# Causal attention with decay and a two-layer mixer on one core: decay rows in the score matmul, exp over whole PSUM banks, mixer groups of 512 tokens

## The chip, the cores and the metric

The program runs on one core of one Trainium2 chip. The time is device time in microseconds (us) from a run of the whole kernel; "the profile" and "the trace" are one execution of it, taken by the hardware profiler. Engines: PE (TensorE: matmul; PEld is its weight load), DVE (VectorE), ACT (ScalarE), POOL (GpSimd, which here mostly issues DMAs) and SP (which issues DMAs too). In both kernels PE writes its results to PSUM tiles of one bank each (128 rows of 512 fp32 columns); the other tiles lie in SBUF. The busy time of an engine is the time in which the profile shows it at work on an instruction.

## The reference, cut to what matters

```python
# q, k, v: (8 batches, 8 heads, 576 tokens, 64); s: (8, 8, 576)
scores = 0.125 * q @ k.T
cum    = cumsum(maximum(s, 0))
scores = where(above_diagonal, -1e9, scores + minimum(-(cum[i] - cum[j]), 0))
x      = softmax(scores) @ v                    # heads side by side: (8, 576, 512)
u      = x + (x.T @ U @ V).T                    # low-rank mix along the tokens, rank 32
out    = u + relu(u @ w_ch1) @ w_ch2            # channel mixer, 512 -> 2048 -> 512
```

576 tokens are 4.5 blocks of 128.

## The kernel before

Attention goes head by head. It is a Python generator, and each `yield` lets the mixer of the *previous two* batches emit one step (mostly four matmuls). Cuts are marked.

```python
NB = 2                                           # the mixer takes two batches at a time
def attention(b):
    for h in range(H):
        # ... load q, k, v of this head ...
        for t in range(NT):                      # NT = 5 token blocks
            if t % 2 == 0:
                yield
            nc.tensor.transpose(qT, q_sd[:M, t, :D], identity[:M, :M])     # weights: M x 64
            nc.vector.tensor_copy(q_aug[:D, ds(t * 128, M)], qT)
            # ... the same for k ...
        for jt in range(5):                      # key blocks
            for (a, csz) in chunks:              # at most 512 queries
                stp = ptmp()
                nc.tensor.matmul(stp[:nk, :csz], lhsT=k_aug[:65, ...], rhs=q_aug[:65, ...])
                if jt % 2 == 0:
                    yield
                if a == jt * 128:
                    nc.vector.tensor_add(stp[:nk, :nk], stp[:nk, :nk], causal_T[:nk, :nk])
                nc.scalar.activation(pT[:nk, :csz], stp[:nk, :csz], EXP,
                                     bias=cum_T[:nk, jt, bh:bh + 1], scale=scale)
                for it in range(i0, i1 + 1):     # value products, at once
                    nc.tensor.matmul(out_ps[it][:M, :65], lhsT=pT[:nk, ds(off, M)],
                                     rhs=v_sb[:nk, jt, :], ...)
        # ... reciprocal on DVE and scaling on ACT, once per token block ...
# main loop: one mixer step for each pause of attention, until the mixer has no more
for yv in attention(b):
    if prev_mix is not None:
        next(prev_mix, None)
```

The mixer gives 94 steps; the attention of two batches pauses 130 times. So the mixer runs dry before the attention does. It also works on 1280 rows for two batches, of which 1152 are tokens.

The softmax here doesn't subtract the row's maximum and nothing guards it: scores larger than these inputs give would overflow.

## Time and profile before

| | before |
|---|---|
| time, median of 4 runs | 767.5 us (767.28 to 767.78) |
| PE / DVE / ACT / POOL busy, % of 768.3 us | 87 / 47 / 45 / 34 |
| time to the first mixer matmul (trace) | 151.0 us |
| from there to the last attention matmul | 526.6 us |
| the rest, mixer alone | 90.7 us |

From the page of the kernel before: busy time, busy tenths of PE in 40 slices, the clock granted to PE in tenths, and the chain of waits by engine and by line (L284 and L299 are the two mixer layers, L203 the value products).

```profile
PE 667.2 (87%) x3637; PEld 305.8 (40%) x3637; DVE 361.2 (47%) x1682; ACT 343.0 (45%) x899; POOL 264.2 (34%) x402
...
PE   0488888899999998889899998889999998889997
...
PEclk9999999999999995559999997558999999559999
...
PE 73%; DVE 10%; ACT 8%; issue 4%; DMA 4%; POOL 1%; ACTq 0%; DVEq 0%; POOLq 0%
PE pa L284 20%; PE pa L299 18%; PE pa L203 14%; ACT pT L191 7%; PE pb L177 6%; PE pb L154 5%; PE pb L158 4%; DMA k_sd<-in_k_dram 3%; PE pa L250 3%; PE pa L237 3%; DVE pb L187 2%; DVE k_aug L159 2%; PE pb L267 2%; DVE k_aug L160 2%; DVE q_aug L155 1%
```

PE is both the busiest engine and the chain. But the row of the clock must be read with care. Where it prints 5, the clock records say half speed: 290 to 345, 471 to 526 and 652 to 693 us. For the first 160 us there is no record, and the row prints 9. Matmuls of 512 columns there start 427 ns apart in the dense places, against 216 ns at recorded full clock, and after a score matmul of 512 columns the next one starts 381 ns later in the median, as in the recorded half-clock stretch from 290 us (382 ns), against 220 ns at full clock. So I read half clock in that stretch too.

From the windows view (busy us and instruction count of each engine, then clock, DMA share, GB/s): attention alone, attention with mixer, and again.

```profile
core 0: us, PE busy (x) PEld busy (x) DVE busy (x) ACT busy (x) POOL busy (x), PEclk, DMA share, GB/s
40.00:120.00 80.00, 65.95 (x386) 33.39 (x385) 49.42 (x274) 48.50 (x139) 49.03 (x76) 1.00 0.56 36
160.00:290.00 130.00, 121.42 (x691) 53.66 (x690) 54.73 (x257) 64.10 (x170) 45.02 (x67) 0.97 0.35 38
290.00:345.00 55.00, 47.18 (x228) 21.30 (x226) 34.26 (x160) 20.94 (x58) 20.23 (x31) 0.50 0.33 22
345.00:471.00 126.00, 117.31 (x684) 52.40 (x683) 54.52 (x255) 63.34 (x167) 45.68 (x67) 1.00 0.36 39
```

In the third line, at half clock, PE is still busy for 86% of the time. Busy does not say at what speed, or how much of it is streaming.

From the groups by shape (rows*columns of the weights, then the moving shape; busy us, mean ns of one, idle before it and its releaser):

```profile
L203 PE MATMUL pa<-v_sb,pT 128*128 128x65 bf16 x640 | 75.5, 219 | 54.9 <-ACT pT L191 51.1
...
L154 PE MATMUL pb<-identity,q_sd 128*64 128x128 bf16 x256 | 64.6, 260 | 15.3 <-DMA q_sd<-in_q_dram 12.5 <-DVE k_aug L159 0.2
...
L203 PE MATMUL pa<-v_sb,pT 128*64 128x65 bf16 x256 | 59.4, 236 | 1.0 <-ACT x_sb L216 0.6
```

Ten value products of a head's fifteen load a full 128x128 square (640 of 960). The rest load 64 columns, and every transpose does. From the waits view (us in total, times, longest us):

```profile
ACT pT L191 <- DVE pb L187: 239.1, 87, 25.3
...
PEld L203 <- ACT pT L191: 106.3, 158, 1.7
...
PE pa L203 <- ACT pT L191: 51.1, 61, 1.2
```

And the timeline of one head at half clock (start, length, what, count, idle before it):

```profile
62.43 1.01 PE L177 MATMUL pb<-q_aug,k_aug 65*128 65x512 bf16 x3
64.40 0.40 PE L203 MATMUL pa<-v_sb,pT 128*128 128x65 bf16 x4 [0.96 <-ACT pT L191]
64.62 0.46 PE L177 MATMUL pb<-q_aug,k_aug 65*128 65x320 bf16 x1
```

Three score matmuls, then about a microsecond of nothing: the value products need the exp of those scores, which needs the mask on DVE.

### The profile page before, as it was taken

To read this page: it belongs to the slowest core of one execution; us is meant where nothing else is said; L and a number is where in the kernel's file an instruction comes from. 1 tells how busy PE (TensorE), PEld (TensorE's weight loads), DVE (VectorE), ACT (ScalarE), POOL (GpSimd) and SP (SyncE) were. 2 spreads that over 40 slices of the span, in tenths; PEclk is the share of its full clock that TensorE was granted. 3 is DMA by queue.
4 is the path that set the end of the run, shared out by engine and by line. 5 is a ranking of instruction groups with operands and counts; after the bars stand their busy time and mean duration, and the time that the engine had idled before them with its cause. 6 is when DMAs were issued, how large, how long until landed. Compare 5 with 4: busy or idle time off the path is not lost.

```text
span 768.3 us, 11729 instructions
## 1 busy us (share of the span) xinstructions
PE 667.2 (87%) x3637; PEld 305.8 (40%) x3637; DVE 361.2 (47%) x1682; ACT 343.0 (45%) x899; POOL 264.2 (34%) x402
## 2 busy tenths in 40 slices
PE   0488888899999998889899998889999998889997
PEld 0244443344444334344344343434444444425543
DVE  4366655744334356664334445574443445662011
ACT  2256566066662325326664244506666333625600
POOL 4666655123243237214333236512333324200000
PEclk9999999999999995559999997558999999559999
DMA  9965555113234335313233344511323434200011
GB/s 167 109 41 36 35 34 34 12 14 24 17 21 61 53 59 44 20 9 24 16 24 43 55 62 48 35 10 12 24 16 25 67 58 55 17 0 1 1 62 62
DMA packets 125582, 28.92 MB, mean 38 GB/s; under 512 B 118128, under 2 KB 120336, under 8 KB 125520
## 3 DMA queue, kind: packets, MB, share of 16 engines
q0 software_dynamic: 119984, 18.45, 32.6%
q1 hardware_dynamic: 5536, 9.74, 3.6%
q8 instruction: 28, 0.46, 0.3%
q14 instruction: 34, 0.28, 0.1%
HBM read 37.07 MB, written 9.51 MB: 61 GB/s over the span
## 4 chain that ended last, share of the span: by engine, by line
PE 73%; DVE 10%; ACT 8%; issue 4%; DMA 4%; POOL 1%; ACTq 0%; DVEq 0%; POOLq 0%
PE pa L284 20%; PE pa L299 18%; PE pa L203 14%; ACT pT L191 7%; PE pb L177 6%; PE pb L154 5%; PE pb L158 4%; DMA k_sd<-in_k_dram 3%; PE pa L250 3%; PE pa L237 3%; DVE pb L187 2%; DVE k_aug L159 2%; PE pb L267 2%; DVE k_aug L160 2%; DVE q_aug L155 1%
## 5 line engine op out<-in xcount | busy, mean ns | idle before, releaser
L191 ACT ACTIVATE pT<-pb,cum_T 128x512 bf16<-128x512 f32 (+5 forms) x384 | 173.3, 479 | 264.8 <-DVE pb L187 239.1
L284 PE MATMUL pa<-uT_sb,w_sb 128*128 128x512 bf16 (+1 forms) x768 | 187.8, 360 | 0.3
L203 PE MATMUL pa<-v_sb,pT 128*128 128x65 bf16 (+2 forms) x960 | 134.8, 225 | 55.9 <-ACT pT L191 51.1
L299 PE MATMUL pa<-w_sb,hT_sb 128*128 128x512 bf16 x640 | 165.8, 384 | 0.0
L203 PEld LDWEIGHTS <-pT 128*128 128x128 bf16 (+2 forms) x960 | 78.3, 110 | 165.6 <-ACT pT L191 106.3
L291 ACT ACTIVATE hT_sb<-pa 128x512 bf16<-128x512 f32 (+1 forms) x192 | 98.4, 526 | 83.1 <-PE pa L284 70.6
L137 POOL DMA_DIRECT2D v_sb<-in_v_dram x64 | 50.4, 787 | 230.8 <-PE pa L203 123.2
L177 PE MATMUL pb<-q_aug,k_aug 65*128 65x512 bf16 (+5 forms) x384 | 109.2, 343 | 0.6
L216 ACT ACTIVATE x_sb<-pa,l_rec 128x64 bf16<-128x64 f32 (+1 forms) x320 | 92.3, 306 | 38.1 <-DVE l_rec L213 26.3
L187 DVE TENSOR_TENSOR pb<-pb,causal_T 128x128 f32<-128x128 f32 (+1 forms) x320 | 82.1, 279 | 49.2 <-PE pb L177 43.2
L137 POOL DMA_DIRECT2D q_sd<-in_q_dram x64 | 50.9, 796 | 155.6 <-PE pb L158 83.7
L213 DVE RECIPROCAL l_rec<-pa 128x1 f32<-128x1 f32 (+1 forms) x320 | 51.2, 161 | 102.5 <-PE pa L203 86.4
L155 DVE COPY q_aug<-pb 64x128 bf16<-64x128 bf16 (+1 forms) x320 | 65.7, 205 | 61.7 <-PE pb L154 52.6
L154 PE MATMUL pb<-identity,q_sd 128*64 128x128 bf16 (+1 forms) x320 | 79.7, 255 | 15.3 <-DMA q_sd<-in_q_dram 12.5
L284 PEld LDWEIGHTS <-w_sb 128*128 128x128 bf16 x768 | 67.4, 100 | 49.8 <-issue 5.4
L159 DVE COPY k_aug<-pb 64x128 bf16<-64x128 bf16 (+1 forms) x320 | 65.8, 206 | 38.1 <-PE pb L158 34.1
L299 PEld LDWEIGHTS <-hT_sb 128*128 128x128 bf16 x640 | 55.9, 98 | 56.8 <-issue 2.0
L158 PE MATMUL pb<-identity,k_sd 128*64 128x128 bf16 (+1 forms) x320 | 76.7, 250 | 0.4
L307 DVE TENSOR_TENSOR o_sb<-u_all,pa 128x512 f32<-128x512 bf16 (+1 forms) x40 | 27.4, 685 | 82.5 <-PE pa L299 81.0
L154 PEld LDWEIGHTS <-q_sd 128*64 128x64 bf16 (+1 forms) x320 | 40.3, 127 | 61.0 <-issue 46.9
L158 PEld LDWEIGHTS <-k_sd 128*64 128x64 bf16 (+1 forms) x320 | 39.4, 125 | 36.4 <-issue 33.9
L137 POOL DMA_DIRECT2D k_sd<-in_k_dram x64 | 52.0, 813 | 1.6 <-issue 0.8
(42 smaller groups left out, 371.1 us busy)
## 6 DMA issues: line engine op xcount, KB each, us to landing
out_dram<-o_sb SPq DMA_DIRECT2D x32, 256.0 KB
w_sb<-in_moe_w_ch_dram POOLq DMA_DIRECT2D x2, 2048.0 KB, 17.8
q_sd<-in_q_dram POOLq DMA_DIRECT2D x64, 64.0 KB, 2.7
k_sd<-in_k_dram POOLq DMA_DIRECT2D x64, 64.0 KB, 2.7
v_sb<-in_v_dram POOLq DMA_DIRECT2D x64, 64.0 KB, 2.7
q_sd<-in_q_dram POOLq DMA_DIRECT2D x64, 8.0 KB, 2.1
k_sd<-in_k_dram POOLq DMA_DIRECT2D x64, 8.0 KB, 2.2
q_aug<-cum_neg_hbm SPq DMA_DIRECT2D x64, 1.1 KB
```

Source lines behind the costliest of these rows:

```text
L137: nc.gpsimd.dma_start(out=dest[:, :4, :D], in_=src[b, h, :512].rearrange("(t p) d -> p t d", p=128),)
L154: nc.tensor.transpose(qT, q_sd[:M, t, :D], identity[:M, :M])
L158: nc.tensor.transpose(kT, k_sd[:M, t, :D], identity[:M, :M])
L159: nc.vector.tensor_copy(k_aug[:D, ds(t * 128, M)], kT)
L177: nc.tensor.matmul(stp[:nk, :csz], lhsT=k_aug[: D + 1, ds(jt * 128, nk)], rhs=q_aug[: D + 1, ds(a, csz)], start=True, stop=True,)
L187: nc.vector.tensor_add(stp[:nk, :nk], stp[:nk, :nk], causal_T[:nk, :nk])
L191: nc.scalar.activation(pT[:nk, :csz], stp[:nk, :csz], EXP, bias=cum_T[:nk, jt, bh : bh + 1], scale=scale,)
L203: nc.tensor.matmul(out_ps[it - it_lo][:M, : D + 1], lhsT=pT[:nk, ds(off, M)], rhs=v_sb[:nk, jt, :], start=(jt == 0), stop=(jt == it),)
L216: nc.scalar.activation(x_sb[:M, it, ds(h * D, D)], out_ps[it - it_lo][:M, :D], COPY, scale=l_rec[:M, :],)
L284: nc.tensor.matmul(f1p[:, :nsz], lhsT=w1_sb[:, kt, ds(nf * 128, 128)], rhs=uT_sb[:, kt, ds(nn, nsz)], start=(kt == 0), stop=(kt == 3),)
L291: nc.scalar.activation(hT_sb[:, nf, ds(nn, nsz)], f1p[:, :nsz], RELU)
L299: nc.tensor.matmul(f2p[:, :d_model], lhsT=hT_sb[:, kt, ds(t2 * 128, 128)], rhs=w2_sb[:, kt, :], start=(kt == 0), stop=(kt == 15),)
```

## The change

The intent is to make attention cheaper in instructions and to keep PE filled.

- Four extra rows of the score matmul carry the decay (the query's as one bf16 row, the key's as a sum of three), instead of one row and a bias per key, so the exp needs no bias and one exp covers a whole PSUM bank of 512 columns from several blocks.
- The mask becomes a bf16 `min` on the exps in SBUF.
- Loads come per batch, and q and k are transposed 128 columns (two tokens) at a time.
- Scores run one pair of heads ahead of the value products.
- The mixer works on nine exact groups of 512 tokens, one after each batch, in steps between the attention steps of the next batch.
- The low-rank product, its residual and the transposes are summed in PSUM.

The diff, cut to its core:

```diff
-            nc.tensor.matmul(stp[:nk, :csz], lhsT=k_aug[: D + 1, ...], rhs=q_aug[: D + 1, ...])
-            nc.vector.tensor_add(stp[:nk, :nk], stp[:nk, :nk], causal_T[:nk, :nk])
-            nc.scalar.activation(pT[:nk, :csz], stp[:nk, :csz], EXP, bias=cum_T[...], scale=scale)
+    KA = D + 4
+            qT = slot[0:KA, hh, 0, :]
+            kT = slot[0:KA, hh, 1, :]
+            diag = pscore()
+            for j in range(4):
+                mm(diag[:, ds(j * 128, 128)], j, j * 128, j * 128 + 128)
+            nc.scalar.activation(pT[:, hh, 0:512], diag, EXP, scale=scale)
+            nc.vector.tensor_tensor(pT[:, hh, 0:512], pT[:, hh, 0:512], keep..., op=ALU.min)
+            mm(tail[:64, ds(hh * 64, 64)], 4, 512, S)
+            yield
+            far = pscore()
+            mm(far[:, 0:448], 0, 128, S)
+            mm(far[:, 448:512], 3, 512, S)
+            nc.scalar.activation(pT[:, hh, 512:1024], far, EXP, scale=scale)
+            # ... mid: blocks 1 and 2, in the same way ...
 ... (value products)
+            for i in range(5):
+                for j in range(i + 1):
+                    kk = 64 if j == 4 else 128
+                    mq = 64 if i == 4 and j in (2, 4) else 128
+                    nc.tensor.matmul(po[:mq, i, :], lhsT=pT[:kk, hh, ds(place(j, i), mq)],
+                                     rhs=vt[:kk, j, h, :], ...)
 ... (order of the whole)
+    drain(transposes(0))
+    load_weights()
+    for n in range(NP + 1):                      # 32 pairs of heads
+        b, hp = divmod(n, PB)
+        if hp == 0 and b + 1 < B:
+            load_qk(b + 1, 1)
+            load_v(b + 1)
+        if n + 1 < NP:
+            run(transposes(n + 1))               # run(): one mixer step after each step
+        if n < NP:
+            run(scores(n))
+        if n > 0:
+            run(values(n - 1))
+            if n % PB == 0:
+                run(seqmix(b - 1))
+                fill.append(chanmix(b - 1))
```

## The prediction

> **What bounds it now.** TensorE. Part 1 of the page: PE busy 667 of 768 us (87%), DVE 47%, ACT 45%. The chain of waits is 73% PE. "Busy" hides three things.
> 1. Clock. The clock records show 0.5 at 290-345, 471-526 and 652-693 us, stretches of attention with no mixer to fill it. Before 160 us there is no record and the page prints full speed; yet 512-column matmuls there last 586-620 ns against 380 ns at recorded full clock, and start every 427 ns against 216. So I read half clock there too: about 310 of 768 us. The Trainium skill, "TensorE: Matmul & The Clock Gate", Part 1, says the array is clocked at half until sustained activity releases it; the trace agrees (attention alone is 0.82 busy with about 1 us waits for exp, the mixed stretches 0.95).
> 2. Columns. The matmul shapes sum to 955k columns; at 216 ns per 512 that is 403 us.
> 3. Weight loads of 64 columns (transposes, last PV row) are followed by 150 ns gaps at full clock, and a 512-column matmul ahead of one takes 310 instead of 216; 128-column loads in PV cost 39. The same page, "Weight-path perf modes", ties the fast load to 128 columns.
>
> **What the change does.**
> - Mixer tokens 5120 padded become 4608 exact: 717k columns to 665k. Attention 238k to 202k (transposes of 72 columns, 128-column weights). Total 867k, 366 us at 216/512: minus 37 us.
> - Attention of batch b is filled by the channel mixer of group b-1: 38 attention steps a batch against 32 mixer steps, so no pure attention except batch 0. PE should stay at full clock from about 65 us on. This is the largest gain.
> - Scores run one pair ahead of values, so PE no longer waits for exp (106 us of PEld waits now).
> - DVE 361 to about 220 us: the mask add on PSUM (82 us) becomes a bf16 min; 640 small transpose copies become 128 of 576 columns, about 0.7 us each; 320 reciprocals become 64. ACT 343 to about 225: 384 exps to 224, x scaling (92 us) leaves ACT. POOL issue 264 to under 90.
> - Adds: decay rows through DRAM, residual as 16 identity matmuls a group; small.
> - Start: weights now load after batch 0 and before batch 1. Weights took 25 us in the trace, small-row loads move about 65 GB/s; estimate: batch 1's q,k land near 53 us while batch 0 finishes near 40, so PE idles 10-15 us.
>
> **Sum (estimate from the durations above).** About 67 us until the first filled batch; remaining attention 27 pairs x 3.7 = 98; seven low-rank stages x 3.6 = 25; nine mixer groups x 28.6 = 257; stalls (normalisation before the low-rank stage, PSUM banks waiting for DVE) about 25; tail 3. **475 us**, range **450 to 520**. Nearly all is on the critical path, since PE is the chain. Chances: faster 0.99, within 2% 0.005, slower 0.005.
>
> **What would show it.** About 3608 matmul records, PE busy near 90% after 70 us, clock 1.0 there; near 51 us a batch; 512-column matmuls every 216 ns; PE idle between about 40 and 55 us, released by DMA of q/k; the last 58 us two dense mixer groups; DVE and ACT under 60%. If the clock records show 0.5 in the mixed stretches, point 1 is wrong; if PE waits on DVE or ACT exceed 40 us, stalls were undersized.
>
> **What would make it wrong.** Half clock returning in the mix (512-column spacing 427): up to +100 us. The start limited by DMA far beyond 55 us. Strided DVE copies much slower than 0.7 us. A pool rotation that serialises score banks.

## The result

The kernel after takes 486.67 us (median of 4 runs, 485.0 to 490.88) against 767.5 us. The ratio is 0.635, 95% interval 0.632 to 0.638. Ratios in this text are the mean time of one kernel's fast runs over that of the other's of the same rounds, so not quite the ratio of the medians. In the experiments both are given against the kernel before in their own rounds.

From the page of the kernel after (L321 and L334 are the mixer layers, L180 scores, L235 value products):

```profile
PE 452.3 (94%) x3608; PEld 255.9 (53%) x3608; DVE 232.1 (48%) x444; ACT 192.4 (40%) x369; POOL 58.9 (12%) x80
...
PE   1195999999999999999999999999999999999996
...
PEclk9999999999999989998999799999999999999999
...
PE 89%; DMA 7%; POOL 2%; DVE 1%; issue 0%; POOLq 0%
PE pwork L321 28%; PE pwork L334 27%; PE pscore L180 11%; PE pwork L235 10%; DMA q_sd<-in_q_dram 6%; PE pwork L159 3%; PE pwork L259 2%; PE pwork L272 2%; PE pwork L280 2%; PE pwork L345 2%; DMA v_slot_93<-in_v_dram 2%; PE pwork L292 1%; PE pwork L300 1%; POOL k_sd L109 1%; POOL q_sd L109 1%
```

PE goes from 87% to 94% of a shorter span, and the chain of waits is 89% PE. The clock row shows 9 almost everywhere. The records behind it show four dips, at 119, 170, 221 and 272 us, of 3.4, 3.4, 3.4 and 6.8 us. The windows view, for the start and for two steady batches:

```profile
core 0: us, PE busy (x) PEld busy (x) DVE busy (x) ACT busy (x) POOL busy (x), PEclk, DMA share, GB/s
...
20.00:44.00 24.00, 19.83 (x164) 13.57 (x164) 12.14 (x28) 13.83 (x28) 6.31 (x8) 1.00 1.22 202
44.00:70.00 26.00, 20.52 (x169) 13.12 (x170) 13.85 (x28) 6.92 (x14) 10.07 (x12) 1.00 2.96 127
114.00:165.00 51.00, 51.00 (x433) 29.23 (x432) 27.41 (x54) 22.59 (x44) 5.07 (x7) 0.97 0.41 57
165.00:217.00 52.00, 52.00 (x437) 29.56 (x434) 28.33 (x55) 22.59 (x44) 6.80 (x9) 0.97 0.41 57
```

From 70 us on, PE never stands idle in this view. The waits of PE that remain are all in the start:

```profile
PE pwork L159 <- DMA q_sd<-in_q_dram: 15.4, 3, 8.3
PE pscore L180 <- DMA slot_118<-rows_hbm: 10.7, 1, 10.7
PE pscore L180 <- DVE slot_119 L164: 0.8, 1, 0.8
```

The groups by shape, for the lines shown of before (the value products are split by buffer; this is one of three):

```profile
L235 PE MATMUL pwork<-v_slot_93,pT 128*128 128x65 bf16 x312 | 21.2, 211 | 0.0
L159 PE MATMUL pwork<-identity,q_sd 72*128 72x72 bf16 x256 | 20.9, 213 | 15.4 <-DMA q_sd<-in_q_dram 15.4
```

The transposes now load 128 columns, and all value products but the last block's two do. A mean of 211 ns says little, since neighbours overlap in the pipeline; what counts is how far apart they start, 29 ns in the median.

A table by stage, from the times of the first mixer matmul and the last value product in the two traces:

| us | before | after |
|---|---|---|
| to the first mixer matmul | 151.0 | 70.0 |
| attention with mixer | 526.6 | 338.6 |
| after the last value product | 90.7 | 74.7 |
| span | 768.3 | 483.3 |

### Where a steady batch's time went

"Busy" cannot say more, so I worked the next table out from the start times of all matmuls. Both traces have a record for every matmul (3637 and 3608, as many as weight loads). The gap from each matmul's start to the next one's start is split in this order:

1. Columns: the moving columns at 2.4 per ns. A 512-column matmul gets 213 ns; the shortest pitch in the traces is 215 to 216. (The Trainium skill, "TensorE: Matmul & The Clock Gate", gives 2.4 GHz as the full clock.)
2. Half clock: as much again where the records say half clock, or before the first record.
3. Change of array shape: where this matmul's weights and the next one's differ in rows or columns (up to 32, up to 64, or more), at most 110 ns of what is left (150 at half clock). Both caps are my choice; at full clock most of these gaps leave 94 to 123 ns beyond the columns (121 to 150 ns after 65 columns, which stream in 27).
4. The rest: waits.

It is taken over four batches from the ends of the first matmul chain of the low-rank stage (317.5 to 679.1 us before, 114.2 to 321.5 us after):

| us per batch | before | after | difference |
|---|---|---|---|
| columns | 49.7 | 41.6 | -8.1 |
| half clock | 7.9 | 2.0 | -5.9 |
| change of array shape | 17.2 | 6.5 | -10.7 |
| other waits | 15.6 | 1.6 | -14.0 |
| sum | 90.4 | 51.8 (rounded parts give 51.7) | -38.6 |

Over the whole span the same split gives, before and after: columns 398 and 361, half clock 79 and 23, changes of shape 126 and 54, waits 147 and 32, before the first and after the last matmul's start 18 and 12.

This is a way of booking time, not yet a proof. A cost booked beside a wait may only hide a longer wait. So the entries were tested.

### The profile page after: what moved, and what is told of

The parts are those of the page before. It is cut to its first block, busy times and chain, and to the rows that moved or that the text cites. A ratio compares the mean times of both kernels' runs of the same rounds, so it can differ in the third digit from the quotient of the medians.

```text
span 483.3 us, 8414 instructions
## 1 busy us (share of the span) xinstructions
PE 452.3 (94%) x3608; PEld 255.9 (53%) x3608; DVE 232.1 (48%) x444; ACT 192.4 (40%) x369; POOL 58.9 (12%) x80
## 4 chain that ended last, share of the span: by engine, by line
PE 89%; DMA 7%; POOL 2%; DVE 1%; issue 0%; POOLq 0%
PE pwork L321 28%; PE pwork L334 27%; PE pscore L180 11%; PE pwork L235 10%; DMA q_sd<-in_q_dram 6%; PE pwork L159 3%; PE pwork L259 2%; PE pwork L272 2%; PE pwork L280 2%; PE pwork L345 2%; DMA v_slot_93<-in_v_dram 2%; PE pwork L292 1%; PE pwork L300 1%; POOL k_sd L109 1%; POOL q_sd L109 1%
## 5 line engine op out<-in xcount | busy, mean ns | idle before, releaser
L321 PE MATMUL pwork<-uT,w_sb 128*128 128x512 bf16 x576 | 146.7, 391 | 0.0
L334 PE MATMUL pwork<-w_sb,hT 128*128 128x512 bf16 x576 | 144.4, 380 | 0.0
L328 ACT ACTIVATE hT<-pwork 128x512 bf16<-128x512 f32 x144 | 86.4, 600 | 106.1 <-PE pwork L321 105.5
L191 ACT ACTIVATE pT<-pscore 128x512 bf16<-128x512 f32 x64 | 38.4, 600 | 145.8 <-issue 89.5
L321 PEld LDWEIGHTS <-w_sb 128*128 128x128 bf16 x576 | 52.1, 100 | 51.2 <-issue 5.0
L334 PEld LDWEIGHTS <-hT 128*128 128x128 bf16 x576 | 49.2, 98 | 45.2 <-issue 1.1
L235 PEld LDWEIGHTS <-pT 128*128 128x128 bf16 (+2 forms) x960 | 54.3, 102 | 24.0 <-issue 0.4
L192 DVE TENSOR_TENSOR pT<-pT,keep 128x512 bf16<-128x512 bf16 x64 | 26.3, 414 | 47.5 <-ACT pT L191 47.5
L200 ACT ACTIVATE pT<-pscore 128x512 bf16<-128x512 f32 x64 | 38.1, 595 | 20.0 <-PE pscore L180 19.0
L180 PE MATMUL pscore<-slot_118 68*128 68x128 bf16 (+5 forms) x198 | 28.5, 266 | 10.7 <-DMA slot_118<-rows_hbm 10.7
L204 ACT ACTIVATE pT<-pscore 128x512 bf16<-128x512 f32 x64 | 38.2, 597 | 0.3 <-PE pscore L180 0.2
L164 DVE COPY slot_119<-pwork 64x576 bf16<-64x576 bf16 x44 | 35.1, 799 | 6.2 <-PE pwork L159 4.6
L164 DVE COPY slot_118<-pwork 64x576 bf16<-64x576 bf16 x44 | 35.2, 799 | 4.5 <-PE pwork L159 3.1
L164 DVE COPY slot_120<-pwork 64x576 bf16<-64x576 bf16 x40 | 32.0, 801 | 4.4 <-PE pwork L159 3.1
L159 PEld LDWEIGHTS <-q_sd 72*128 72x128 bf16 x256 | 17.4, 108 | 27.8 <-DMA q_sd<-in_q_dram 16.1
L245 DVE TENSOR_TENSOR x_sb<-pwork,rec 128x320 bf16<-128x320 f32 x64 | 31.1, 490 | 2.0
L180 PE MATMUL pscore<-slot_119 68*128 68x128 bf16 (+5 forms) x198 | 28.6, 263 | 0.8 <-DVE slot_119 L164 0.8
L180 PEld LDWEIGHTS <-slot_118 68*128 68x128 bf16 (+1 forms) x198 | 16.5, 105 | 23.0 <-issue 12.4
L235 PE MATMUL pwork<-v_slot_93,pT 128*128 128x65 bf16 (+1 forms) x360 | 27.2, 214 | 0.0
```

The lines of the kernel that those rows point to most:

```text
L159: nc.tensor.transpose(tp[:, c, t2, :], src[:, h, ds(t2 * 128, 128)], identity[:TP, :TP])
L164: nc.vector.tensor_copy(dst[:, :, :, :, par], tp[par * D : par * D + D].rearrange("p c t m -> p c m t"),)
L180: nc.tensor.matmul(dst, lhsT=kT[:, ds(j * 128, min(128, S - j * 128))], rhs=qT[:, lo:hi], start=True, stop=True,)
L191: nc.scalar.activation(pT[:, hh, 0:512], diag, EXP, scale=scale)
L192: nc.vector.tensor_tensor(pT[:, hh, 0:512], pT[:, hh, 0:512], keep.rearrange("p a b -> p (a b)"), op=ALU.min)
L200: nc.scalar.activation(pT[:, hh, 512:1024], far, EXP, scale=scale)
```

## The experiments

All kernels gave correct results. Those on the kernel before are named b, those on the kernel after a. In most of their traces one or two per cent of the matmul records are missing (3546 of 3608, say), so only medians of gaps and whole times are read from them, not sums of gaps.

The theories:

- F: unfilled attention, at half clock, is what cost the time (my prediction called this the largest gain).
- V: the wait of the value products for exp costs.
- S: changes of the array shape cost.
- My prediction's point 3: the narrow load itself costs.

### b1_paced: the mixer spread evenly over the attention

```diff
+            owed += 94
+            if owed >= 130:
+                owed -= 130
                 if prev_mix is not None:
                     next(prev_mix, None)
```

> The kernel before, with one thing changed: the mixer advances on 94 of each 130 attention steps instead of on every one until it runs dry, so that it lasts through both batches. Theory F (unfilled attention is what costs: half clock and waits): the recorded half-clock stretches of about 55 us at the end of each pair of batches vanish or shrink below 15 us each, each of the three loses 15 to 25 us, total 690 to 720 us. Rival W (attention is slow by its own waits and instruction count, wherever the mixer stands): within 2% of 767 us, the waits merely move.

Measured: 774.69 us, ratio to before 1.008 (1.006 to 1.010). So it is slower, not some 50 to 75 us faster. From its page, and its waits view:

```profile
PE   0488888898889999888889998988898999989997
...
PEclk9999999999999999757999899966999999979999
```

```profile
PE pa L203 <- ACT pT L191: 47.4, 68, 1.2
```

The long half-clock stretches did shorten: the records between the first one and 700 us hold 109 us of half clock instead of 157. But shorter dips spread over the rest, and the waits for exp stayed. The rival W was right for this kernel. There are 94 steps for 130 pauses, and moving them does not make more of them. In a form that blames the clock alone, theory F fell here.

The split fits this. About 310 us of the kernel before run at half clock, but it books only 79 us of them to the clock, as the matmuls there stream few columns. It charges the clock with streaming alone, though. If half clock also delays the work that waits for a matmul's end, that stands under waits, so 79 us may be too little.

### b2_fullshape: transposes with full 128x128 weights

```diff
-                qT = qp.bitcast(BF16)[:D, :M]
-                nc.tensor.transpose(qT, q_sd[:M, t, :D], identity[:M, :M])
-                nc.vector.tensor_copy(q_aug[:D, ds(t * 128, M)], qT)
+                qT = qp.bitcast(BF16)[:128, :128]
+                nc.tensor.transpose(qT, q_sd[:, t, :], identity)   # q_sd: 128 columns, 64 of them 0
+                nc.vector.tensor_copy(q_aug[:D, ds(t * 128, M)], qT[:D, :M])
```

> The kernel before, with one thing changed: q and k lie in 128-column tiles padded with zeros, so that each transpose loads 128 x 128 weights instead of 128 x 64, 64 x 64. Same matmul count, 8192 more moving columns (3.4 us at full clock), nothing else. Summing in the trace of before what each change of the array shape between neighbouring matmuls cost over the streaming time gives 126 us, 63 of them beside a transpose. Theory S (small array shapes cost time where they meet full ones): 710 to 740 us. Rival C (only columns and waits count): 767 to 775 us.

Measured: 748.79 us, ratio 0.976 (0.972 to 0.980), 20 us less in the medians. That lies outside both forecasts. The direction is that of theory S: more columns, and less time. But 63 us had been booked beside transposes, and 20 came back. The same split of its trace (1.4% of the matmul records are missing) books 84 us to changes of shape against 126, so only 42 us of them went, since transposes still meet other small shapes. Some 5 us came back as half clock, 3 as columns, and the rest as waits. Which waits was not shown; b5_first_full below speaks against the one for exp. And this edit widens the load and removes changes at once: it can't tell theory S from my point 3.

### b3_scoresfirst: a head's scores and exps before its value products

```diff
                         pT = sb.tile([128, 512], BF16, tag="pT", bufs=12)
                         nc.scalar.activation(pT[:nk, :csz], stp[:nk, :csz], EXP, ...)
-                        for it in range(i0, i1 + 1):      # value products
-                            ...
+                        done.append((jt, a, csz, pT))
+                for jt, a, csz, pT in done:
+                    for it in range(i0, i1 + 1):
+                        ...
```

> The kernel before, with one thing changed: a head's six score matmuls and exps all come before its value products (pT gets 12 buffers), with the same eight pauses per head at which the mixer may step. This takes the wait of the first value product for its exp away (L203 behind ACT, 50 us of gaps after 160 us, some 70 in all), which neither pacing nor full shapes touched. Theory V (that wait bounds attention in the kernel before): 690 to 730 us. Rival: it only moves to the PSUM banks or to DVE, 755 to 775 us.

Measured: 710.55 us, ratio 0.925 (0.924 to 0.927), 57 us less. From its waits view:

```profile
PE pb L177 <- ACT pT L191: 29.9, 32, 2.5
...
PE pa L209 <- ACT pT L191: 3.0, 12, 0.6
```

The value products (now L209) no longer wait for exp to speak of. Part of the wait moved to the scores, which now wait for a PSUM bank that ACT has not emptied yet. Theory V holds, and this is the largest single step found from the side of the kernel before. The cut above leaves out that the five PSUM banks of the value products are now asked for after the scores, and that the pauses stand at other places; what these two did was not separated.

### b5_first_full and b6_all_three: together

b5_first_full has the edits of b3 and b2. b6_all_three has the edit of b1 as well.

> b3_scoresfirst and b2_fullshape together. b2 alone gained 19 us although its changes of shape lost 42 us of cost: the rest turned into waits. If the wait for exp is what swallowed it, together they gain more than the sum of both alone, 640 to 690 us. If the two simply add, about b3 minus 19 us.

> b5_first_full with the pacing of b1. b1 alone lost 0.8%. If pacing needs a dense attention to pay (theory F in a weaker form), it now gains 15 us or more over b5_first_full and half-clock records between 200 and 690 us fall under 40 us. If the amount of filling and not its place decides, within 1% of b5_first_full.

Measured: b5 687.58 us, ratio 0.896 (0.894 to 0.897); b6 674.28 us, ratio 0.877 (0.874 to 0.880). For b5, b2's edit is worth 23 us beside b3 against 20 alone. They nearly add; the expected help of one for the other is too small to claim, so the wait for exp is not what swallowed b2's gain. For b6, pacing alone lost 0.8%, and now it gains 13 us (1.9%), a little under the 15 us that theory F's weaker form asked for, and more than the 1% of its rival. Its trace has 66 us of recorded half clock, b5's 138; between 200 and 690 us it has 59, where under 40 were forecast. In an attention that waits less, pacing pays a little.

### a1_nofill: the kernel after, each mixer group in one piece

```diff
-                fill.append(chanmix(b - 1))
+                drain(chanmix(b - 1))
```

> The kernel after, with one thing changed: each channel mixer group is issued in one piece after its batch, not in steps between attention steps. Look-ahead of scores, shapes and columns stay. Theory F: the clock records show half clock in the attention stretches, a batch takes 61 to 66 us instead of 49.6, total 565 to 605 us. Rival L (the look-ahead and the fewer instructions had already made attention dense): under 505 us.

Measured: 554.91 us (550.97 to 563.99), ratio 0.719 (0.716 to 0.723). That is 67 to 68 us slower than the kernel after, and a little under the expected range. From the windows view, mixer group, attention with the low-rank stage, mixer group, attention in turn:

```profile
core 0: us, PE busy (x) PEld busy (x) DVE busy (x) ACT busy (x) POOL busy (x), PEclk, DMA share, GB/s
72.00:100.50 28.50, 28.34 (x142) 13.42 (x145) 2.85 (x5) 9.44 (x16) 0.18 (x1) 1.00 0.44 41
100.50:130.60 30.10, 29.56 (x293) 19.03 (x290) 24.23 (x50) 13.38 (x28) 5.88 (x7) 0.67 0.61 71
130.60:161.00 30.40, 30.08 (x142) 13.83 (x145) 2.50 (x4) 9.55 (x16) 0.00 (x0) 0.94 0.07 26
161.00:194.20 33.20, 32.82 (x293) 21.38 (x290) 24.39 (x50) 13.84 (x28) 5.87 (x7) 0.56 0.57 64
```

Look at the clock, the third number from the right: 1.00 and 0.94 while the mixer runs, 0.67 and 0.56 while attention runs alone, with PE 98 to 99% busy in all four. The records give the steps: half clock from 110.6 us, 10 us after attention began alone, to 134.5 us, 4 us after the mixer had come back, and again from 165.2 to 199.3 us. The records hold 174 us of half clock against 18 in the kernel after. The split of this trace (0.7% of the matmul records are missing) books 80 us to half clock against 23, 61 to changes of shape against 54, and 44 to waits against 32. So here, where attention hardly waits any more, filling is worth its 68 us, and most of that is the clock. Theory F was right about this kernel. It is not shown for the step from before to after, where 94 of 130 pauses had been filled already.

The Trainium skill, "TensorE: Matmul & The Clock Gate", Part 1, says that the clock is released by sustained activity. These traces agree, and they show that the profile's "busy" is not that activity.

### a6_nolook: values right after their own pair's scores

```diff
-        if n > 0:
-            run(values(n - 1))
+        if n < NP:
+            run(values(n))
```

(The low-rank stage moves by one pair with it.)

> The kernel after, with one thing changed: values of a pair follow right after its own scores instead of one pair later. The fill stays. If the fill alone covers the wait for exp: within 2% of 487 us. If the look-ahead was needed: about 1 us of wait in each of 32 pairs, 510 to 525 us.

Measured: 484.31 us, ratio 0.628 (0.625 to 0.631); the kernel after had 0.635 in its own rounds. The look-ahead of one pair is not needed: without it, too, the waits view of PE shows no wait for exp. Four steps of scores for two heads stand before the first value product in either order, with mixer steps between, and I take this coarser order to be what removed the wait. b3 supports it from the other side; the kernel after was not run without it.

### a5_exps: one exp per score matmul again

```diff
-            nc.scalar.activation(pT[:, hh, 0:512], diag, EXP, scale=scale)
+            for j in range(4):
+                nc.scalar.activation(pT[:, hh, ds(j * 128, 128)], diag[:, ds(j * 128, 128)], EXP, scale=scale)
```

(In the same way two exps each for `far` and `mid`.)

> The kernel after, with one thing undone: each exp covers one score matmul instead of a whole PSUM bank, 8.5 a head instead of 3.5. ACT gains about 80 us of busy time (192 to some 270 of 487 us). ACT is off the chain of waits, so: within 1% of 487 us. If the bank-wide exp carries part of the gain: 495 us or more.

Measured: 486.46 us, ratio 0.634 (0.632 to 0.636), the same as the kernel after. From its page:

```profile
PE 448.0 (93%) x3553; PEld 255.3 (53%) x3608; DVE 233.5 (48%) x444; ACT 209.9 (43%) x689; POOL 58.9 (12%) x80
```

ACT has 320 instructions more, and is busy for 210 us instead of 192. I had expected 270; the durations of its instructions do add up to 277 us, but they overlap. The exp over whole banks is off the chain and brings nothing by itself.

### a0_again and a2_narrow: load or change of shape?

a0_again is the kernel after, unchanged, as the yardstick for the next three.

> The kernel after, unchanged, on the chip of the next three runs, as their yardstick: 485 to 491 us.

Measured: 487.5 us (485.18 to 494.83), ratio 0.634 (0.633 to 0.635).

```diff
-                    mq = 64 if i == 4 and j in (2, 4) else 128
+                    mq = 64 if i == 4 and j > 0 else 128
```

> The kernel after, with one thing changed: in the value product of the last row block, the loads for j = 1 and 3 have 64 columns too, so four loads of a head are narrow instead of two, but they now stand together: three changes of array shape instead of four. My prediction's point 3 (each narrow load is slow, 150 ns instead of 39): two more narrow loads x 64 heads x about 0.1 us = 10 to 15 us longer. Theory S (the change of shape costs, about 110 ns each, whatever the load): 64 x 0.1 = 5 to 8 us shorter.

Measured: 480.68 us, ratio 0.6247 (0.6227 to 0.6266), against 0.6341 (0.6326 to 0.6355): 1.5% *faster* with twice as many narrow loads. From its groups of weight loads by shape (mean ns of one is the last number before the bar):

```profile
L235 PEld LDWEIGHTS <-pT 128*128 128x128 bf16 x704 | 32.3, 102 | 14.3 <-issue 0.4
...
L235 PEld LDWEIGHTS <-pT 128*64 128x64 bf16 x192 | 11.4, 114 | 3.7
```

The narrow load is 12 ns longer on average. Medians of the gap from one value product to the next at full clock in this trace: full to full 29 ns; full to 128x64 123; 128x64 to 128x64 52 after the first of a run and 35 after the second; 128x64 to 64x64 124; 64x64 to full 147. So a narrow matmul among its like costs 6 to 23 ns more than a full one (35 - 29, 52 - 29), and each *change* costs 72 to 118 ns (124 - 52, 147 - 29). My point 3 took the neighbours' cost for the load's own.

The Trainium skill says so, in a page that I had not looked up: "TensorEngine Tiling (Array Packing)", Key Properties, "Changing tiling mode (not just tile) drains the TensorE". It gives no figure. The traces agree and give one, if a load of at most 64 rows or columns counts as another mode, which is my reading: the traces show shapes, not modes. The 6 to 23 ns would fit the same page's Restrictions, by which column tiling turns off the fast weight load; no run here tests that.

### a3_onesize: every matmul in the full array

Every small shape left is padded with zeros. The padded shapes load over 64 rows and 128 columns. No moving column is added.

```diff
-    U_sb = consts.tile([128, 5, R], BF16)
-    V_sb = consts.tile([R, S], BF16)
+    U_sb = consts.tile([128, 5, 128], BF16)      # zero beyond column 32
+    V_sb = consts.tile([128, S], BF16)           # zero beyond row 32
-    slots = [consts.tile([128, 2, 2, S], BF16, ...)]
+    slots = [consts.tile([128, 2, 2, 640], BF16, ...)]   # zero beyond 576
-                    kk = 64 if j == 4 else 128
-                    mq = 64 if i == 4 and j in (2, 4) else 128
+                    kk = mq = 128                # pT laid out so that 128 columns can be read
-                lhsT=x_sb[:64, 4, ds(dt * 128, 128)],
-                rhs=identity[:64, :64],
+                lhsT=x_sb[:, 4, ds(dt * 128, 128)],
+                rhs=identity[:, :64],
 ... (score tail and low-rank stage in the same way; the front's two fp32 tiles share the room of
      a mixer buffer, to make place)
```

> The kernel after, with every remaining small array shape padded with zeros to over 64 rows and 128 columns (last block of the value product, score tail, U and V of the low-rank stage, residual of the last 64 tokens). No moving column is added or removed. In the trace of after the changes of shape cost 54 us over the streaming time, of which some 6 in the cold start. Theory S: 430 to 445 us, and after 70 us nearly every matmul starts at its columns/2.4 GHz. Rival C: 485 to 495 us.

Measured: 430.46 us, ratio 0.560 (0.558 to 0.562), 57 us less than a0_again in the medians. From its page and its windows view (one batch):

```profile
PE 387.0 (90%) x3546; PEld 229.9 (54%) x3608; DVE 233.2 (54%) x452; ACT 190.9 (45%) x369; POOL 59.1 (14%) x83
...
PE   1286289999999999999999999999999999999996
...
PEclk9999999999999999999999999999999999999999
```

```profile
core 0: us, PE busy (x) PEld busy (x) DVE busy (x) ACT busy (x) POOL busy (x), PEclk, DMA share, GB/s
...
151.00:194.00 43.00, 42.39 (x426) 25.42 (x433) 27.76 (x54) 22.41 (x44) 5.97 (x8) 1.00 0.49 69
```

A batch takes 43.3 us now (the low-rank stages lie 43.2 to 43.3 us apart), of which 41.6 are columns. In the steady batch the 8.5 us gained (51.8 to 43.3) are the 6.5 booked to changes of shape and the 2.0 booked to the dips of the clock. So here what was booked came back in full. No wait stood beside it to swallow it. The four dips of the clock are gone too: the records show full clock from 68 us to 429 us. That the changes of shape caused the dips is likely but not shown: the order of the work is the same, but the layout of the exps and some buffers changed too. The 2.0 us a batch that they cost were not separated from the rest.

### a4_order: the load order of the start

```diff
             load_qk(b + 1, 1)
+            if b == 0:
+                load_mixer(1)                    # w_ch1
             load_v(b + 1)
+            if b == 0:
+                load_mixer(2)                    # w_ch2
```

(Both weights leave `load_weights`, so q and k of batch 1 come before them.)

> The kernel of a3_onesize, with the load order changed: q and k of batch 1 before the first mixer weight, v of batch 1 before the second. The wait of PE for q at 43 to 49 us goes and the first filled step moves from 70 to about 55 us: 10 to 18 us shorter than a3_onesize. If the total bytes of the start bound it instead (the weights then come late), under 5 us.

Measured: 417.58 us, ratio 0.543 (0.541 to 0.544), 13 us less than a3_onesize. The wait of PE for q, in a3_onesize and then in a4_order:

```profile
PE pwork L167 <- DMA q_sd<-in_q_dram: 21.1, 4, 10.5
```

```profile
PE pwork L171 <- DMA q_sd<-in_q_dram: 9.9, 2, 8.6
```

The first mixer matmul starts at 56.1 us instead of 69.2. From there to the last value product both take 287 us. So the gain is the start's alone, as expected. This is the best version found: 46% less than the kernel before, 14% less than the kernel after (0.5428 over 0.6341).

## Why the prediction was right or wrong

**The time: right.** 475 us were predicted with a range of 450 to 520, and 486.67 measured. Of the 12 us missed, 3 are the start (70.0 for 67), some 6 the steady batches (51.8 us for near 51, about seven times), and the rest lies between the profiled span of 483.3 us and the median time. Two terms were off in opposite directions. A batch of the sum (4 x 3.7 + 3.6 + 28.6 = 47.0 us) stands 5.4 us above the 41.6 us of columns, where changes of shape and dips of the clock took 8.5 (6.5 and 2.0 in the split). Waits in the mixed stretch were set at 25 us and were near 11 (1.6 times seven). In all 9.0 us a batch were set beside the columns and 10.1 taken; that the two errors nearly cancel is luck. That the time came right although the ranking of the gains below did not is no luck: the 475 us were added up from durations of the parts at full clock, and no estimate of what filling would save enters the sum.

**The start: right.** 67 us to the first filled batch were predicted, 70.0 measured. PE was to stand idle at 40 to 55 us for q and k; it did at 43 to 48.7 us, for `q_sd`. That is under 6 us where 10 to 15 were expected, so the total of the start came nearer than its parts. a4_order shows that the order of loads costs 13 us (in the padded kernel).

**The load of the other engines: right in kind.** DVE 232 us (about 220 predicted), ACT 192 (225), POOL 59 (under 90). But a5_exps shows that the ACT part brings nothing, as it lay off the chain.

**"This is the largest gain": not so for the clock, open for the filling as a whole.** Point 1 read the half clock rightly, in place and in length, and then took length for cost. Of the 310 us at half clock the split books 79 to the clock, and of the 285 us gained by the profiled runs 56, in the steady batch 5.9 of 38.6. Two other entries are larger: waits (14.0 of 38.6; b3 alone gained 57 us by removing the one for exp) and changes of shape (10.7 of 38.6). More even filling of the kernel before bought nothing (b1_paced: 0.8% slower), while the kernel after loses 68 us without its filling (a1_nofill), more than by any other single undoing that was tried. But a mixer beside attention also covers waits. In the kernel before, the 55 us without mixer (290 to 345 us) hold 14.0 us of waits in the split and the 126 us with it (345 to 471 us) 17.4. How many of these went by filling, and how many by the order of scores and values, was not separated.

**"Scores run one pair ahead of values, so PE no longer waits for exp": right in effect, wrong in cause.** The wait is gone, and it is gone without the look-ahead too (a6_nolook). Grouping the scores before the values does it in the kernel before (b3_scoresfirst), and probably here.

**Point 3, narrow loads: wrong cause.** The 150 ns gaps are there, but they belong to the change of array shape. Twice as many narrow loads with one change fewer ran 1.5% faster (a2_narrow). The right cause also says what the wrong one can't: that the 32x128 loads of the low-rank stage, which are not narrow, need padding too: the median gap from such a matmul to its neighbour of another shape is 131 ns after 64 columns and 307 to 317 after 512 in the kernel after, and 29 and 216 ns in a3_onesize.

**Columns: right.** 955k to 867k columns, predicted to be worth 37 us; the split has 398 to 361.

What stays open: the step from b6_all_three (674 us) to the kernel after (487 us) was not divided by experiments. It holds the fewer columns (the 37 us), filling from the first batch on instead of after two (81 us less until the first mixer matmul), the small shapes left in b6, and fewer instructions. These overlap and cannot simply be added up. The split of b6's trace (1.5% of the records missing, some 12 us of columns, which it counts as waits) books about 138 us to waits once those are taken off, against 32 in the kernel after; so most of the 187 us stands there. The largest that the waits view of PE names is 30.7 us of scores waiting for PSUM banks that exp has not emptied. The kernel before has three banks for scores and transposes together, the kernel after four for scores and four for the rest; that difference was not tested. Nor was the busy share found at which the clock is released.

## What to carry to other kernels

Split the gaps between matmul starts into streamed columns, clock, changes of array shape and waits before saying what PE is busy with, and then test each entry: in a kernel that waits, a booked cost comes back only in part (b2: 20 of the 42 us that went), in one that streams, in full (a3). Give neighbouring matmuls one array shape, with zeros if need be, for padding rows and weight columns costs no streaming time. Put a head's scores and exps before its value products, and load what the next stage needs before weights that are needed later.

## What the Trainium skill lacked or had wrong

- "TensorEngine Tiling (Array Packing)", Key Properties, states the drain at a change of mode without a figure. Here, beyond the 27 ns that 65 columns stream: about 97 ns from the full array into 128x64 (a gap of 123 to 124 ns), about 120 ns back from 64x64 (147 ns). Rows of 68 or 72 beside 128 cost nothing (gaps of 33 ns after 72 columns and 82 ns after 192, which stream in 30 and 80).
- "TensorE: Matmul & The Clock Gate" does not mention that drain where it recommends shapes for small matmuls; removing all changes was worth 57 of 487 us here, dips of the clock included.
- The same page, Back-to-back issue gap, gives a sustained 131 ns for 512 columns and 81 ns for 128 with weight loads between, and calls 216 and 56 ns the gap of isolated matmuls, which other parts of the page measure back to back. Here each has its own load, and the medians in the stream are 216 and 56 ns, and the fastest tenth of the 512-column gaps is at 215.
- The same page, Part 1, ties the clock to how busy PE has been, but does not say that this is not what the profile calls busy. Here attention alone, with PE 98 to 99% busy, fell to half clock after 5 to 10 us, in all seven such stretches, and got the full clock back between 3 us before (in the low-rank stage) and 5 us after the mixer returned (a1_nofill); the kernel before had half clock at 86% busy.
- No page says that the profile's clock row prints full speed where it has no record. Here that hid half clock in the first 160 us of 768 (427 ns between 512-column matmuls, not 216).
